# Batch 0's output projection as seven products of 256 columns per group of four feature blocks, with the orders dealt anew

## The chip, the cores and the metric

One Trainium2 chip, one core. The metric is the device time of one execution in microseconds (us): the median of 3 runs of the kernel before is 738.43 us (738.42 to 738.86).

## The reference

```python
B, H, S, Ns, D = (8, 8, 512, 32, 64)          # x: B,H,S,D   state: B,H,Ns,D
scores = scale * np.matmul(x, state.transpose(0, 1, 3, 2))
a = softmax(scores);  xread = np.matmul(a, state)
scores2 = scale * np.matmul(state, x.transpose(0, 1, 3, 2))
a2 = softmax(scores2); sread = np.matmul(a2, x)
attn_out = np.concatenate([xread, sread], axis=2)
x = attn_out.transpose(0, 2, 1, 3).reshape(B * S, H * D)    # S is 512 + 32 here
rms = np.sqrt(np.mean(x * x, axis=-1, keepdims=True) + 1e-06)
xn = x / rms * rms_g
g = xn @ w_gate                                # 512 x 1536
silu = g * (1.0 / (1.0 + np.exp(-g)))
out = (silu * (xn @ w_val) @ w_out)            # 1536 x 512
```

Tokens read from the states (cross attention), states read from the tokens, an RMS norm, and a gated feed-forward network. The three weight matrices arrive as float64; x, state and the output are float32.

## The kernel before

**Work.** A batch has 512 tokens; its 1536 hidden features are 12 feature blocks of 128, taken in six pairs `mp`. Because the tokens read from only 32 states per head, a pair's gate and value weights are first multiplied with the states (L745: "own weights", tile `v`), and the hidden layer is then a product of these with the attention weights `aT_s`. For batch 0 that is done plainly, block by block in `hidden`: two PSUM tiles `pv` for a block (L791 for block 0, in halves of 256 columns, L798 for the others, 512 columns), a silu on ScalarE into `t` (L804) and a product on VectorE into `hb` (L808). The pool of `pv` has two buffers, so a block's products need the tiles that the silu and the product of the block before have read. Batch 0's output projection is `project_as_ready`, L1005: each of the 12 blocks of `hb` times `wo`, for four rows of 128 tokens, 512 columns each, accumulated in four PSUM banks over all 12 blocks. `projected` copies these banks out on ScalarE (L1022). Batches 1 to 7 and the states use products by Strassen's scheme: seven in place of eight for the hidden layer (`hidden_seven`, L902, 256 columns each), 49 in place of 64 for the projection (`project_twice`, L1206). Their sums of weights are made at the end of batch 0's stage: `weight_sums` (L1048) and `weight_quarters` (L1160), both on VectorE; the sums of `v` (`vs`, L772 to L775) and of `aT_s` (`aT_t`, L820 to L823) are made on GpSimd.

**Weights.** The 18 pieces of 1 MB (gate, val, out for each pair in turn) are loaded by SyncE (L235), RAW_AHEAD of them ahead, and become float32 by two ScalarE passes (`lin` L268, `ex` L271, in `exponents`) and two VectorE passes (L292, L296, in `values`). The end of a piece's VectorE passes frees its buffer and issues the load of the piece RAW_AHEAD later. Gate and val of a pair go into a tile `w_m` and from there to `w_d` in DRAM, from which the later batches fetch them; the third goes to its place in `wo`.

**Order.** Every instruction's place on its engine is fixed by strings written out by hand. Each letter of such a string takes one step of a generator: in ORDER, `h`, `t`, `u` are the three parts of `hidden` for batch 0, `p` the projection, `c` its copies, `e` and `d` the two halves of the conversion, `v` the products with the states, `A` and `S` batch 1's attention, `s` the states' read of batch 0 (L629 to L699), `k` `weight_sums`, `Q` quarters, `w` batch 1's first products, `z` a matmul that only keeps TensorE awake (L1346). FIRST holds batch 1, PERIOD batches 2 to 6, LAST batch 7, STATES the states. Engines run their own queues in order and wait for one another by semaphores; `ORDER` covers about the first 124 us.

The tables `seven["c22"]`, `seven["s2"]` and `seven["k"]` are pools for the later batches' projection that are opened late, in the space that the pools of the startup (`raws`, `conv`, `x_0`) leave.

## Time and profile before

| | |
|---|---|
| median of 3 runs | 738.43 us |
| profiled execution, its own time | 738.43 us |
| span of its instructions | 736.5 us |
| granted TensorE clock | 1.000 |
| TensorE busy | 730.9 us (99%) |
| VectorE busy | 564.6 us (77%) |
| ScalarE busy | 350.2 us (48%) |
| GpSimd busy | 271.4 us (37%) |

Rows of the profile give a start and a length in us (timeline, chain of waits), or a stretch and then each engine's busy time in it with its number of instructions (windows). PE is TensorE, PEld its weight load, DVE VectorE, ACT ScalarE, POOL GpSimd, SP SyncE. A float32 matmul that the program writes once stands as two TensorE instructions in the trace: the 48 matmuls of L1005 are 96 there. A name after "<-" in brackets is what ended the idle time before the instruction.

### The profile page before, as it was taken

The numbers are of one execution on the slowest core, as the hardware profiler recorded it, in microseconds if no ns is written. First come the engines' busy times: TensorE is split into PE (matmuls) and PEld (weight loads), VectorE is DVE, ScalarE is ACT, GpSimd is POOL, SyncE is SP. The second block draws the span as 40 slices with busy tenths as digits, with TensorE's granted clock in tenths as the row PEclk, the third lists the DMA queues.
The fourth block names the chain that finished last, engine by engine and source line by source line (L and its number), as shares of the span: only waits on it lengthen the run. The fifth ranks groups of instructions, "written<-read, shape, count | busy, mean of one in ns | idle before, by whom it ended". The sixth has DMA issues, their size and how long they took to land.

```text
span 736.5 us, 14288 instructions
## 1 busy us (share of the span) xinstructions
PE 730.9 (99%) x5604; PEld 591.4 (80%) x5604; DVE 564.6 (77%) x952; ACT 350.2 (48%) x610; POOL 271.4 (37%) x362
## 2 busy tenths in 40 slices
PE   9999999999999999999999999999999999999997
PEld 7644444889978997789888987899778987899996
DVE  5885697799848994699569984899469955888852
ACT  5997923563275426553455427542655336411220
POOL 2300006521482228512753248222851277325400
PEclk9999999999999999999999999999999999999999
DMA  8989946917682297507861588229850782063411
GB/s 235 367 284 378 325 179 241 330 52 267 213 321 58 95 319 278 168 30 304 270 228 29 212 283 304 61 93 321 281 165 31 301 278 75 1 231 114 143 44 29
DMA packets 58426, 146.15 MB, mean 198 GB/s; under 512 B 10228, under 2 KB 29176, under 8 KB 51448
## 3 DMA queue, kind: packets, MB, share of 16 engines
q1 hardware_dynamic: 47312, 126.30, 48.3%
q10 hardware_dynamic: 11048, 18.95, 8.6%
q8 instruction: 44, 0.72, 0.4%
q14 instruction: 22, 0.18, 0.1%
HBM read 116.46 MB, written 28.77 MB: 197 GB/s over the span
## 4 chain that ended last, share of the span: by engine, by line
PE 98%; DMA 1%; SPq 0%; issue 0%; ACT 0%
PE f L902 40%; PE f L1206 31%; PE f L1005 6%; PE pv L798 5%; PE pv L745 4%; PE f L1068 2%; PE at L745 2%; DMA x_b<-in_x_dram 1%; PE at L450 1%; PE f L672 1%; PE at L368 1%; PE pv L791 0%; PE at L319 0%; PE at L672 0%; PE f L577 0%; PE pv L529 0%
## 5 line engine op out<-in xcount | busy, mean ns | idle before, releaser
L902 PE MATMUL f<-aT_s,v 128*128 128x256 f32 x504 | 118.8, 381 | 0.0
L902 PEld LDWEIGHTS f<-aT_s,v 128*128 128x128 f32 x504 | 94.9, 191 | 19.3 <-issue 5.3
L965 DVE TENSOR_TENSOR g<-g,f 128x512 f32<-128x512 f32 x84 | 56.1, 683 | 60.8 <-PE f L902 54.5
L1234 POOL TENSOR_TENSOR kept<-kept 128x256 f32<-128x256 f32 x28 | 24.4, 872 | 171.5 <-DVE kept L1246 112.7
L902 PE MATMUL f<-aT_t,vs 128*128 128x256 f32 x336 | 86.7, 382 | 0.0
L1206 PE MATMUL f<-w,h 128*128 128x128 f32 x588 | 75.4, 276 | 0.0
L1206 PEld LDWEIGHTS f<-w,h 128*128 128x128 f32 x588 | 70.1, 192 | 4.1 <-issue 4.1
L902 PEld LDWEIGHTS f<-aT_t,vs 128*128 128x128 f32 x336 | 62.6, 190 | 13.2 <-issue 3.1
L772 POOL TENSOR_TENSOR vs<-v 128x256 f32<-128x256 f32 x42 | 33.0, 785 | 106.7 <-ACT v L757 106.5
L1219 ACT COPY kept<-f 128x512 f32<-128x512 f32 (+1 forms) x56 | 29.3, 545 | 81.5 <-PE f L1206 58.1
L956 ACT ACTIVATE hb<-g 128x1024 f32<-128x1024 f32 x42 | 44.5, 1059 | 46.2 <-DVE g L965 46.1
L312 POOL TENSOR_TENSOR ri<-ss,mhalf 128x4 f32<-128x4 f32 (+1 forms) x9 | 9.8, 1094 | 109.8 <-ACT ss L400 104.6
L954 ACT COPY g<-f 128x512 f32<-128x512 f32 x42 | 24.6, 585 | 49.0 <-PE f L902 49.0
L757 ACT COPY v<-pv 128x512 f32<-128x512 f32 x56 | 31.0, 595 | 31.9 <-PE pv L745 31.6
L978 DVE TENSOR_TENSOR hb<-hb,f 128x512 f32<-128x512 f32 (+1 forms) x48 | 31.0, 645 | 18.1 <-PE f L902 17.8
L1005 PE MATMUL f<-wo,hb 128*128 128x512 f32 x96 | 44.1, 599 | 0.0
L902 PE MATMUL f<-aT_t,v 128*128 128x256 f32 x168 | 43.8, 383 | 0.0
L902 PE MATMUL f<-aT_s,vs 128*128 128x256 f32 x168 | 43.2, 380 | 0.0
L965 DVE TENSOR_TENSOR c<-c,f 128x512 f32<-128x512 f32 (+1 forms) x48 | 31.2, 650 | 15.1 <-PE f L902 15.0
L1206 PE MATMUL f<-wo,h 128*128 128x128 f32 x336 | 42.1, 275 | 0.0
L1206 PE MATMUL f<-wo,hb 128*128 128x128 f32 x336 | 42.1, 275 | 0.0
L1206 PEld LDWEIGHTS f<-wo,hb 128*128 128x128 f32 x336 | 39.9, 192 | 0.5
(242 smaller groups left out, 1621.3 us busy)
## 6 DMA issues: line engine op xcount, KB each, us to landing
w_m<-w_d SPq DMA_DIRECT2D x48, 1024.0 KB
w<-t_d SPq DMA_DIRECT2D x49, 576.0 KB
out_dram<-kept SPq DMA_DIRECT2D x28, 256.0 KB
raw<-in_moe_w_val_dram SPq DMA_DIRECT2D x6, 1024.0 KB
raw<-in_moe_w_out_dram SPq DMA_DIRECT2D x6, 1024.0 KB
w_d<-w_m SPq DMA_DIRECT2D x6, 1024.0 KB
x_b<-in_x_dram SPq DMA_DIRECT2D x6, 1024.0 KB
x_d<-xB ACTq DMA_DIRECT2D x6, 1024.0 KB
```

What stands on the lines that cost most here:

```text
L745: TE.matmul(out=pv[e][Ns * j:Ns * j + Ns, :], lhsT=stT_g[b][D * e:D * e + D, j, :], rhs=w[D * e:D * e + D, j].rearrange("p m k f -> p (m k ...
L757: SE.copy(v[:, e].rearrange("p m k f -> p (m k f)"), pv[e])
L772: GE.tensor_tensor(out=vs[:, 0], in0=a21, in1=a22, op=ALU.add)
L798: TE.matmul(out=to[0], lhsT=lhs(i, k), rhs=r, start=(i == 0), stop=(i == len(rhs) - 1))
L902: TE.matmul(out=ps[:, i, 0:half], lhsT=l[:, i, :], rhs=r, start=(start and i == 0 and k == 0), stop=(k == len(lhs) - 1), skip_group_check= ...
L954: SE.copy(gates(q)[1], q["x"][:, :, 0:half])
L956: SE.activation(out=hb[:, 2 * mp:2 * mp + 2, 0:n].rearrange("p m (c t) -> p m c t", c=2), in_=q["g"][:, :, :, 0:half], func=ACTF.Silu if s ...
L965: VE.tensor_tensor(out=to, in0=to, in1=q[ps][:, :, 0:half], op=ALU.add)
L978: VE.tensor_tensor(out=part, in0=part, in1=val, op=ALU.mult)
L1005: TE.matmul(out=banks[r], lhsT=hb[:, m, P * r:P * r + P], rhs=wo[:, m, :], start=(m == 0), stop=(m == NM - 1))
L1206: TE.matmul(out=to[half][:, slot, :], lhsT=lhs[:, k, :], rhs=rhs[:, k, :], start=(fresh and n in (0, 4) and k == 0), stop=(k == QM - 1), s ...
L1219: SE.copy(of_half(k, i), banks[name][i])
```

## The change

Batch 0's projection no longer runs block by block. The conversion and the hidden layer of batch 0 take the pairs in the order 0, 3, 1, 4, 2, 5 (`BLOCKS`), so that after every second pair four feature blocks are there which form a group g: blocks 2g, 2g+1 and 6+2g, 7+2g. For each of the three groups the projection is made by seven products of four matmuls each (21 products, 84 matmuls of 256 columns in place of 48 of 512); a letter of the order takes two of the four. Three of the seven go to the banks "11", "12", "21" and accumulate there over the groups. Four go one after another into one bank, "x", whose content is wanted after each of them: for group 0 ScalarE copies it out (L1075), for groups 1 and 2 VectorE adds it to what was kept (L1077). The four sums of weights of a group are made by 12 subtractions on GpSimd (L1023), one of which overwrites a quarter of `wo`; the four sums of `hb` by 12 operations on VectorE (L1033). `weight_sums` then has 9 operations in place of 12. At the end VectorE makes three sums from PSUM and GpSimd two more, and the output is stored in four pieces of 128 x 2 x 256. RAW_AHEAD is 3, `lin` has one buffer, and `en` lies in the tile "kept". ORDER, PERIOD and FIRST are dealt anew; LAST and STATES stay.

```diff
 P = 128
-RAW_AHEAD = 4
+RAW_AHEAD = 3
 W_BUFS = 3
+BLOCKS = (0, 3, 1, 4, 2, 5)
...
 ORDER = (
-    "zzzzaazaaaaggggaaazzzbzeeeaaabddaaabbeeddbbbbsssbzaaaAAAAabbdbeaaaaabAbbbAAAAAdb"
...
+    "zzzzaazaaaggggaaaaziizzbzeeeaaaddbbebbaddaabebbsssebzaaaAAAAaAAssabbdAAssdbabbaa"
...
 PERIOD = (
-    "vxahthththuhuhuthththhthhvvhaaaxxhhxxafaauuuutttuhhthhaahhuuuuttxhuhhthhauukkath"
...
+    "vahhntthhhtuuhhhnutttaahhhhaxtxvvaahhuuuaxxhuuttxthhhhthhxhaaauuuuauthfuthxxutkx"
...
 FIRST = (
-    "aaaaahtvvqqqqqqqqahathhhvtuqquxxhhtqhuhxqthutthuuhhaaahauxttqhtfuxxxhhqqhhthxuuu"
...
+    "hhaattavqvhxtaxhahhaauuuqtuqhhtqqtvhqhthhquuqquahuthtqqfuaxhhutxxqqxhthhuaahuhhu"
...
+    seven["k"] = ctx.enter_context(tc.tile_pool(name="kept", bufs=1))
+    seven["c22"] = ctx.enter_context(tc.tile_pool(name="late2", bufs=2))
+    seven["s2"] = ctx.enter_context(tc.tile_pool(name="quarters_h", bufs=2))
...
     conv = early.enter_context(tc.tile_pool(name="conv", bufs=2))
+    line = early.enter_context(tc.tile_pool(name="line", bufs=1))
...
     pieces = []
-    for mp in range(NM // 2):
+    for mp in BLOCKS:
...
         if kind == 2:
+            mp = BLOCKS[mp]
...
                     tops[k] = conv.tile([P, 8 * P], I32, name="ex")
-                    lin = conv.tile([P, 8 * P], F32, name="lin")
+                    lin = line.tile([P, 8 * P], F32, name="lin")
...
                     if k % 3 == 1:
-                        nc.sync.dma_start(out=w_d[k // 3], in_=w_sb[k // 3])
+                        nc.sync.dma_start(out=w_d[BLOCKS[k // 3]], in_=w_sb[k // 3])
...
         yield
-        en = x_0.tile([P, HT, 2, 4 * Ns], F32, name="en")
-        e = eS.rearrange("p c e j n -> p (c e j) n")
-        VE.tensor_tensor(out=en.rearrange("p c e (j n) -> p (c e j) n", n=Ns), in0=e,
-                         in1=z.unsqueeze(2).to_broadcast(e.shape), op=ALU.mult)
+        if "en" not in soft_0:
+            soft_0["en"] = seven["k"].tile([P, 2, HT, HD], F32, name="kept", tag="kept")
+        en = soft_0["en"][:, h]
+        VE.tensor_tensor(out=en.rearrange("p c (k n) -> p (c k) n", n=Ns),
+                         in0=eS.rearrange("p c e j n -> p (c e j) n"),
+                         in1=z.unsqueeze(2).to_broadcast([P, HT * 2 * 4, Ns]), op=ALU.mult)
...
             for c in range(HT):
-                TE.transpose(out=tp[:, i, c, :], in_=en[:, c, i, :], identity=ident)
+                TE.transpose(out=tp[:, i, c, :], in_=en[:, c, P * i:P * i + P], identity=ident)
...
-    def project_as_ready(banks):
-        for f in (fx, fz, fx, fy):
-            banks.append(f.tile([P, DM], F32, name="f"))
-        def part(m, r):
-            TE.matmul(out=banks[r], lhsT=hb[:, m, P * r:P * r + P], rhs=wo[:, m, :],
-                      start=(m == 0), stop=(m == NM - 1))
-        for m in range(NM - 2):
-            for r in range(4):
-                part(m, r)
-                if r % 2:
-                    yield
-        for r in range(4):
-            part(NM - 2, r)
-            part(NM - 1, r)
-            yield
+    def wo_block(g, i, j):
+        return wo[:, HM * i + 2 * g:HM * i + 2 * g + 2, HD * j:HD * j + HD]
+    def hb_block(g, i, j):
+        return hb[:, HM * j + 2 * g:HM * j + 2 * g + 2, HS * i:HS * i + HS]
+    GROUPS = HM // 2
+    group_t, group_s = {}, {}
+    def group_weights():
+        for g in range(GROUPS):
+            t = group_t[g] = seven["s2"].tile([P, 3, 2, HD], F32, name="group", tag="h2")
+            b11, b12, b21, b22 = (wo_block(g, i, j) for i in range(2) for j in range(2))
+            for to, x_, y_ in ((t[:, 0], b12, b11), (t[:, 1], b22, t[:, 0]), (b12, b22, b12),
+                               (t[:, 2], b21, t[:, 1])):
+                GE.tensor_tensor(out=to, in0=x_, in1=y_, op=ALU.subtract)
+                yield
+    def group_tokens():
+        for g in range(GROUPS):
+            u = group_s[g] = seven["s2"].tile([P, 3, 2, HS], F32, name="group", tag="h2")
+            a11, a12, a21, a22 = (hb_block(g, i, j) for i in range(2) for j in range(2))
+            for to, x_, y_, op in ((u[:, 0], a21, a22, ALU.add), (u[:, 1], u[:, 0], a11, ALU.subtract),
+                                   (a21, a11, a21, ALU.subtract), (u[:, 2], a12, u[:, 1], ALU.subtract)):
+                VE.tensor_tensor(out=to, in0=x_, in1=y_, op=op)
+                yield
+    def group_product(bank, lhs, rhs, start, stop):
+        for k in range(2):
+            for r in range(HT):
+                TE.matmul(out=bank[:, r, :], lhsT=lhs[:, k, P * r:P * r + P], rhs=rhs[:, k],
+                          start=(start and r == 0 and k == 0), stop=(stop and k == 1),
+                          skip_group_check=True)
+            yield
+    def groups_direct(banks):
+        for name, pool in (("11", fx), ("12", fz), ("21", fx)):
+            banks[name] = pool.tile([P, HT, HD], F32, name="f")
+        for g in range(GROUPS):
+            first, last = g == 0, g == GROUPS - 1
+            yield from group_product(banks["11"], hb_block(g, 0, 1), wo_block(g, 1, 0), first, last)
+            yield from group_product(banks["12"], group_s[g][:, 2], wo_block(g, 1, 1), first, last)
+            yield from group_product(banks["21"], hb_block(g, 1, 1), group_t[g][:, 2], first, last)
+    def groups_chained(banks):
+        x_ = banks["x"] = fy.tile([P, HT, HD], F32, name="f")
+        for g in range(GROUPS):
+            yield from group_product(x_, hb_block(g, 0, 0), wo_block(g, 0, 0), True, True)
+            yield from group_product(x_, group_s[g][:, 1], group_t[g][:, 1], False, True)
+            yield from group_product(x_, hb_block(g, 1, 0), wo_block(g, 0, 1), False, True)
+            yield from group_product(x_, group_s[g][:, 0], group_t[g][:, 0], False, True)
+    kept_0 = []
+    def chained_sums(banks):
+        k = seven["k"].tile([P, 2, HT, HD], F32, name="kept", tag="kept")
+        kept_0.extend([k[:, 0], k[:, 1]] + [seven["c22"].tile([P, HT, HD], F32, name="c22") for i in range(2)])
+        for g in range(GROUPS):
+            for k in kept_0:
+                if g == 0:
+                    SE.copy(k, banks["x"])
+                else:
+                    VE.tensor_tensor(out=k, in0=k, in1=banks["x"], op=ALU.add)
+                yield
     def projected(banks, store):
-        spare = seven["s"].rearrange("p (r k) f -> p r (k f)", r=3)
-        for r in range(4):
-            ot = spare[:, r] if r < 3 else two.tile([P, DM], F32, name="ot", tag="g")
-            SE.copy(ot, banks[r])
-            store(r, 0, DM, ot)
-            yield
+        k11, k12, k21, k22 = kept_0
+        VE.tensor_tensor(out=k11, in0=k11, in1=banks["11"], op=ALU.add)
+        store(0, 0, HD, k11)
+        yield
+        VE.tensor_tensor(out=k12, in0=k12, in1=banks["12"], op=ALU.add)
+        yield
+        GE.tensor_tensor(out=k12, in0=k12, in1=k21, op=ALU.subtract)
+        VE.tensor_tensor(out=k21, in0=k21, in1=banks["21"], op=ALU.add)
+        store(1, 0, HD, k21)
+        yield
+        store(1, HD, HD, k22)
+        GE.tensor_tensor(out=k12, in0=k12, in1=k22, op=ALU.add)
+        store(0, HD, HD, k12)
+        yield
...
         seven["vs"] = ctx.enter_context(tc.tile_pool(name="sums", bufs=3))
-        seven["c22"] = ctx.enter_context(tc.tile_pool(name="late2", bufs=2))
         seven["w2"] = ctx.enter_context(tc.tile_pool(name="quarters_w", bufs=3))
-        seven["s2"] = ctx.enter_context(tc.tile_pool(name="quarters_h", bufs=2))
-        seven["k"] = ctx.enter_context(tc.tile_pool(name="kept", bufs=1))
...
                 return wo[:, HM * i + k:HM * i + k + 2, HD * j:HD * j + HD]
-            for dst, a, b in ((t1[:, k:k + 2], blk(0, 1), blk(0, 0)),
-                              (t2[:, k:k + 2], blk(1, 1), t1[:, k:k + 2]),
-                              (blk(0, 1), blk(1, 1), blk(0, 1)),
-                              (t4[:, k:k + 2], blk(1, 0), t2[:, k:k + 2])):
-                VE.tensor_tensor(out=dst, in0=a, in1=b, op=ALU.subtract)
+            for dst, a, b, op in ((t2[:, k:k + 2], blk(0, 1), blk(0, 0), ALU.add),
+                                  (t1[:, k:k + 2], blk(1, 1), t2[:, k:k + 2], ALU.subtract),
+                                  (t4[:, k:k + 2], blk(1, 0), t2[:, k:k + 2], ALU.subtract)):
+                VE.tensor_tensor(out=dst, in0=a, in1=b, op=op)
...
             if b == 0:
-                rows_ = rows_.rearrange("(h p c) f -> h c p f", h=2, c=HT)
-                nc.sync.dma_start(out=rows_[r // HT, r % HT], in_=ot)
+                rows_ = rows_.rearrange("(h p c) f -> h p c f", h=2, c=HT)
+                nc.sync.dma_start(out=rows_[r], in_=ot)
...
             if m not in parts_0:
-                parts_0[m] = hidden(m, lambda e, k, m=m: v_sb[0, m // 2][0][:, e, m % 2, k, :],
+                parts_0[m] = hidden(2 * BLOCKS[m // 2] + m % 2, lambda e, k, m=m: v_sb[0, m // 2][0][:, e, m % 2, k, :],
...
-    parts_0, banks_0 = {}, []
+    parts_0, banks_0 = {}, {}
...
                "h": of_batch_0(0), "t": of_batch_0(1), "u": of_batch_0(2),
-               "p": project_as_ready(banks_0), "c": projected(banks_0, store_tokens(0)),
+               "p": groups_chained(banks_0), "r": groups_direct(banks_0), "W": group_weights(),
+               "T": group_tokens(), "x": chained_sums(banks_0), "c": projected(banks_0, store_tokens(0)),
...
         for stream in ORDER:
-            if stream in "ckw" and "s" not in seven:
+            if stream in "kw" and "s" not in seven:
...
```

Three places show what moved. The first is ScalarE's queue ahead of batch 0's first silu (L804, now L812). `xT` and `aT_s` are the tokens and the attention weights, `e` the exponentials of batch 0's states' read (L636, now L644). Before:

```order
L271 ACTIVATE ex<-lin,bounds 128x1024
L593 COPY aT_s<-at 128x2x256
L343 COPY xT<-at 128x4x128 x3
L593 COPY aT_s<-at 128x2x256
L268 ACTIVATE lin<-raw,bounds 128x1024
L757 COPY v<-f 128x512 x2
L271 ACTIVATE ex<-lin,bounds 128x1024
L804 ACT_TABLE_LOAD
L804 ACTIVATE t<-pv 128x512
```

and now:

```order
L349 COPY xT<-at 128x4x128
L644 ACTIVATE e_361,z_364<-sS,s_362 128x512
L656 COPY e_361<-at 128x512
L274 ACTIVATE lin<-raw,bounds 128x1024
L765 COPY v<-f 128x512
L277 ACTIVATE ex<-lin,bounds 128x1024
L601 COPY aT_s<-at 128x2x256
L765 COPY v<-f 128x512
L274 ACTIVATE lin<-raw,bounds 128x1024
L277 ACTIVATE ex<-lin,bounds 128x1024
L812 ACT_TABLE_LOAD
L812 ACTIVATE t<-pv 128x512
```

Ahead of the silu there now also stand the two exponentials of the states' read (one of them is the row just above the first one shown), a copy of them and one more pair of conversion passes.

The second is TensorE's queue in the middle of the stage, where a pair's products with the states (L745, now L753) are followed by hidden products (L798, now L806) and projection. Before:

```order
L745 MATMUL at<-w_m,stT_g 32x512 x8
L1005 MATMUL f<-wo,hb 128x512 x2
L798 MATMUL pv<-aT_s,v 128x512 x8
L745 MATMUL at<-w_m,stT_g 32x512 x8
L1005 MATMUL f<-wo,hb 128x512 x6
L450 MATMUL at<-aT_s,rows 64x512 x4
L450 MATMUL pv<-aT_s,rows 64x512 x4
L1005 MATMUL f<-wo,hb 128x512 x2
```

and now:

```order
L1039 MATMUL f<-wo,hb 128x256 x4
L753 MATMUL at<-w_m,stT_g 32x512 x8
L1039 MATMUL f<-wo,hb 128x256 x2
L1039 MATMUL f<-group 128x256 x4
L1039 MATMUL f<-wo,group 128x256 x4
L1039 MATMUL f<-wo,hb 128x256 x4
L1039 MATMUL f<-group,hb 128x256 x4
L806 MATMUL pv<-aT_s,v 128x512 x2
L1039 MATMUL f<-group 128x256 x4
```

The projection's products stand in lots of 2 or 4 matmuls, half a product or a whole one; those with `group` need the sums of GpSimd and VectorE, and those of bank "x" need it to have been read.

The third is VectorE's queue late in the stage, with the quarters of weights (L1160, now L1226), the products into `hb` (L808, now L816) and the large sum for batch 1's tokens (L463, now L469). Before:

```order
L1048 TENSOR_TENSOR wt<-wo,wt 128x512
L1160 TENSOR_TENSOR w_1033<-wt,w_1033 128x384 x2
L1160 TENSOR_TENSOR wt<-wt 128x3x128
L808 TENSOR_TENSOR hb<-t,pv 128x512
L1160 TENSOR_TENSOR w_1041<-wt 128x384
L1160 TENSOR_TENSOR w_1041<-wt,w_1041 128x384 x2
L808 TENSOR_TENSOR hb<-t,pv 128x512
L1160 TENSOR_TENSOR wt<-wt 128x3x128
L463 TENSOR_TENSOR aT_s<-aT_s,at 128x1024
```

and now:

```order
L1226 TENSOR_TENSOR w_1048<-wt,w_1048 128x384
L1077 TENSOR_TENSOR kept<-kept,f 128x512
L816 TENSOR_TENSOR hb<-t,pv 128x512 x2
L1033 TENSOR_TENSOR group<-hb 128x512
L1033 TENSOR_TENSOR group<-group,hb 128x512
L1033 TENSOR_TENSOR hb<-hb 128x2x256
L694 TENSOR_SCALAR sr<-at,z_751 128x64 x2
L1033 TENSOR_TENSOR group<-hb,group 128x512
L469 TENSOR_TENSOR aT_s<-aT_s,at 128x1024
L1082 TENSOR_TENSOR kept<-kept,f 128x512
L1077 TENSOR_TENSOR kept<-kept,f 128x512
```

Between the quarters and that sum there now stand the last group's four operations on `hb` and the additions from the banks.

More of the change, by code (lines that the diff above doesn't have):

```diff
@@ L26 @@
 ORDER = (
[L27 to L31 removed]
+    "zzzzaazaaaggggaaaaziizzbzeeeaaaddbbebbaddaabebbsssebzaaaAAAAaAAssabbdAAssdbabbaa"
+    "AaAsbbssvbabbebavebbvAddeAehbdhtdeeAAuAdddhAAethuvvveephtddsssWhuesehhssreddstpA"
+    "xdvveeWWWuTTrTppxTrrpvpeerrhxppddWAAAAeeddthhAeAAeddStddvvdvhhhuWWxiueppAeeAAddA"
+    "tuhheAddrtuTAeeArxTATTApApeSddSSvxrAvAAvrAppihxShAedppWtheeeuhetdxdvvvddupkkWWWk"
+    "kkkkSSShrrSSthhtAAQQQQkpQQxAWuhuTTTSSTAAwrrcppwwwwwxwQQrrSkcpSprrxcQppxwQwcQQ"
 )
 PERIOD = (
[L35 to L38 removed]
+    "vahhntthhhtuuhhhnutttaahhhhaxtxvvaahhuuuaxxhuuttxthhhhthhxhaaauuuuauthfuthxxutkx"
+    "hhtuuhkkutvxkuahhhxxtthaahhuaaathushhuuuuhtthassthhthguuuuuutuuuspphupupcpkkppck"
+    "kkklkskkgppppppkkpkffkaakaaaapppgfkpcakppppppppcckpgagkppcaakaaakskppaoaaakkkkkg"
+    "ppppppppppaaapgkkoaaoopaassssakkkkppppaapkpkosacwwxxwxxsssxflfcooxo"
 )
 FIRST = (
[L42 to L46 removed]
+    "hhaattavqvhxtaxhahhaauuuqtuqhhtqqtvhqhthhquuqquahuthtqqfuaxhhutxxqqxhthhuaahuhhu"
+    "ttthhhqhtxxuukqhkaquuGuvtxhhtaaaukxtaaaGhhtkhhxxhhhGuuuuuttutaaauhhuhuhtuhuutupp"
+    "hppppppaaaucuffupkakukkkkppcpppkkpkpppckkaakaalaakkkkkpfkpppcpassaaksaagsppcpkpk"
+    "akkkppggappppppppaoogggpsssgcppkakkpssppkooaaassppkskppakkkkoopaafpwwxxxclfwxsxx"
+    "coos"
 )
```

11 lines of the change are left out of this document (removed).

## The prediction

> **What bounds the kernel now.** I read the page's busy shares and its chain of waits first, then busy time by stage, then the chain in order of time around the projection.
>
> ```profile
> PE 730.9 (99%) x5604; PEld 591.4 (80%) x5604; DVE 564.6 (77%) x952; ACT 350.2 (48%) x610; POOL 271.4 (37%) x362
> PE 98%; DMA 1%; SPq 0%; issue 0%; ACT 0%
> 0.00:26.50 26.50, 24.81 (x201) 19.55 (x201) 15.58 (x45) 17.11 (x29) 6.93 (x27) 1.00 0.85 266
> 26.50:123.80 97.30, 97.30 (x484) 43.02 (x483) 76.44 (x119) 67.60 (x90) 13.34 (x21) 1.00 0.79 289
> 123.80:203.60 79.80, 79.80 (x670) 68.03 (x675) 65.99 (x112) 37.20 (x67) 27.95 (x37) 1.00 0.66 227
> 522.70:602.48 79.78, 79.78 (x671) 68.32 (x677) 63.73 (x106) 37.51 (x71) 35.18 (x46) 1.00 0.59 197
> 676.90:736.50 59.60, 55.72 (x421) 53.08 (x419) 32.43 (x60) 12.35 (x29) 12.68 (x13) 1.00 0.20 71
> ```
>
> TensorE sets the end: 99% of the span and 98% of the chain. The five lower rows are stages, each with its length and then the busy time of PE, PEld, DVE, ACT and POOL. From 26.5 us, where batch 0's hidden layer begins, to 123.8 us, where batch 1's begins, TensorE has no idle time at all; nor in batch 1 (the third row) or batch 6 (the fourth). So a TensorE microsecond taken out of the second row is a microsecond of the end, as long as the others bring their operands in time; and a changed order of batches 1 to 6 has nothing to win there. The second engine of the stage is VectorE, with 97.3 - 76.4 = 20.9 us of idle time. The profiled execution took 738.43 us, the median of the runs too, so the sum is made against 738.43.
>
> **TensorE's work.** The chain gives the pitch of the old product and of the new one's shape, which batches 1 to 7 use for their hidden layer:
>
> ```profile
> 33.80 5.15 PE f L1005 x12
> 131.51 15.87 PE f L902 x72
> 149.26 15.74 PE f L902 x72
> ```
>
> Each matmul of the program is two instructions here. Before: 48 matmuls, 96 x 5.15/12 = 96 x 0.429 = 41.2 us. After: 84 matmuls are 168 instructions of 256 columns, 168 x 15.74/72 = 168 x 0.2186 = 36.7 us. **-4.5 us.** Bounds: by the slower row 168 x 0.2204 = 37.0, so -4.2; the windows' third row has batch 1's 168 such instructions, in a stage without idle time, and nothing there makes them cheaper than 36.1 (0.215), so -5.1. The columns fall from 48 x 512 to 84 x 256, by an eighth, and TensorE is given no instruction of another kind, so nothing hides this term.
>
> **The start.** ScalarE's queue ahead of the first silu:
>
> ```profile
> 18.43 0.58 ACT L343 COPY xT<-at 128x512 f32<-128x512 f32 x1 [0.30 <-PE at L341]
> 22.27 1.07 ACT L343 COPY xT<-at 128x512 f32<-128x512 f32 x2 [0.57 <-PE at L341]
> 24.22 0.58 ACT L593 COPY aT_s<-at 128x512 f32<-128x512 f32 x1 [0.87 <-PE at L591]
> 29.45 0.60 ACT L804 ACTIVATE t<-pv 128x512 f32<-128x512 f32 x1 [0.17 <-PE pv L791]
> 29.94 1.25 ACT L268 ACTIVATE lin<-raw,bounds 128x1024 f32<-128x1024 int16 x1
> 31.22 1.15 ACT L271 ACTIVATE ex<-lin,bounds 128x1024 int32<-128x1024 f32 x1
> 37.31 0.72 ACT L636 ACTIVATE e<-sS,s 128x512 f32<-128x512 f32 x1
> 42.59 1.07 ACT L648 COPY e<-at 128x512 f32<-128x512 f32 x2
> 30.10 0.30 PEld L798 LDWEIGHTS pv<-aT_s,v 128*128 128x128 f32 x2 [0.23 <-ACT t L804]
> 41.72 1.04 PE L646 MATMUL at<-ident,e 128*128 128x128 f32 x8
> ```
>
> The new order puts four kinds of work of batch 0 and the conversion ahead of that silu: two exponentials (2 x 0.72), one copy of them (1.07/2 = 0.53) and one pair of conversion passes (1.25 + 1.15), 4.4 us. ScalarE's idle time there is 0.30 + 0.57 + 0.87 + 0.17 = 1.9 us. So the silu starts some 2.5 us later, and the ninth row says who waits: block 1's products need the PSUM tile that it empties. Of this, half of the eight transposes of the tenth row (0.5 us) are TensorE work done earlier. **+2.0 us.** From below 0 (the queue ahead of 17 us has room for all of it); from above 3.9 (none of the idle time takes it in). I stay at the row sum, give or take 0.9, its largest single wait.
>
> **VectorE and GpSimd.** Prices:
>
> ```profile
> L1048 DVE TENSOR_TENSOR wt<-wo x3: 681/681/683, 95.6 to 101.1; 128x512 f32<-128x512 f32 x3
> L1022 ACT COPY hs<-f x3: 585/585/587, 116.7 to 122.2; 128x512 f32<-128x512 f32 x3
> L710 POOL TENSOR_TENSOR sqT<-sqT x2: 1052/1162/1273, 636.5 to 637.8; 128x512 f32<-128x512 f32 x1, 128x256 f32<-128x256 f32 x1
> 113.47 0.55 DVE L1160 TENSOR_TENSOR wt<-wt 128x384 f32<-128x384 f32 x1
> 119.34 1.08 DVE L1160 TENSOR_TENSOR wo<-wo 128x384 f32<-128x384 f32 x1
> 115.23 0.73 POOL L820 TENSOR_TENSOR aT_t<-aT_s 128x256 f32<-128x256 f32 x1 [3.01 <-DVE aT_s L463]
> 118.96 1.04 POOL L772 TENSOR_TENSOR vs<-v 128x256 f32<-128x256 f32 x1
> 131.99 1.04 POOL L774 TENSOR_TENSOR v<-v 128x256 f32<-128x256 f32 x1
> 132.37 0.67 DVE L965 TENSOR_TENSOR g<-g,f 128x512 f32<-128x512 f32 x1
> ```
>
> VectorE gains 12 sums of `hb`, 8 additions from bank "x" and 3 from the others, and loses 3 weight sums: 20 x 0.68 = 13.6 us, into 20.9 us of idle time. ScalarE gains four copies and loses four (0.585 each): nothing. GpSimd gains 12 subtractions of 512 elements at 1.27 us, 15.2 us, where it is idle for 97.3 - 13.3 = 84 us; two more at the end. By themselves these fit. But the last six rows show the two engines hindering each other: an operation of 384 elements with both inputs in SBUF takes 0.55 us while GpSimd is idle and 1.08 beside a GpSimd addition, which itself goes from 0.73 to 1.04. With one input in PSUM (L965) VectorE keeps its 0.67 beside L774. So the 15.2 us of GpSimd work become up to 15.2 x 1.04/0.73 = 21.7 us, in which VectorE runs at 0.55/1.08 = 0.51 and loses up to 10.6 us. The stage will be 97.3 - 4.5 + 2.0 = 94.8 us. With nothing lost VectorE needs 76.4 + 13.6 = 90.0 of it, with half of that loss 95.3, with all 100.6. About half of VectorE's work in this stage has two SBUF inputs (the `or` of the conversion, the sums of weights and of `hb`), so I take the half: **+0.5 us**, with 0 below (work slips into batch 1's stage, where VectorE has 79.8 - 66.0 = 13.8 us free) and +5.8 above.
>
> The Trainium skill has a stricter rule for these pairs: SBUF — State Buffer, section "Who interferes with whom", says that a VectorE instruction with two SBUF inputs and a GpSimd instruction that reads SBUF exclude each other, and the loser is blocked for the other's whole instruction; with at most one SBUF input VectorE doesn't contend. The trace agrees on who suffers (1.08 against 0.67), not on a block by the whole 1.04 or more. By that rule alone, with each subtraction met, VectorE would lose 15.2 us, need 105.2, and the time be 738.43 - 4.5 + 2.0 + 10.4 = 746.3 (an estimate); it is the far end of the second rival below, and I give it 0.03 of that rival's chance.
>
> **The chained bank.** Each of the twelve products into "x" waits until the one before has been read. On TensorE most have other work between; the shortest cover that I find, one of the other seven products with its four matmuls, is 8 x 0.2186 = 1.75 us against a read-out of 0.59 (ScalarE) or 0.68 us (VectorE) behind what its queue holds, at worst one conversion pass:
>
> ```profile
> 93.88 1.22 DVE L296 TENSOR_TENSOR wo<-raw,ex 128x1024 int32<-128x1024 int32 x1
> ```
>
> 1.22 + 0.68 = 1.90, a shortfall of 0.15 that may come at a few places. Price 0 in the sum, since ScalarE's four reads and most of VectorE's have the queue free; from above 12 x 0.6 = 7.2, with every read-out exposed.
>
> **Loads.** With RAW_AHEAD 3 a piece is asked for when the piece three before is done. One load, alone on the queues, is issued at 73.05, and the DMA share falls back in the last window:
>
> ```profile
> 73.05 0.37 SPq L235 DMA_DIRECT2D raw<-in_moe_w_gate_dram  x1
> 73.00:74.00 1.00, 1.00 (x4) 0.52 (x3) 0.59 (x1) 0.37 (x1) 0.00 (x0) 1.00 0.04 16
> 77.00:78.00 1.00, 1.00 (x7) 0.69 (x6) 0.85 (x2) 0.98 (x3) 0.00 (x0) 1.00 0.46 176
> ```
>
> That is some 4.4 us from issue to landing. The pieces of the conversion follow each other every 4 to 6 us (18 in some 95 us), so three buffers leave two pitches, 8 us or more: 0, hidden by ScalarE's other work; at worst the tightest piece late by a microsecond or two, inside the next term's risk. One `lin` buffer keeps a pass from starting before the one that reads it is over, 0.1 us a piece, in ScalarE's 97.3 - 67.6 = 29.7 us of idle time: 0. FIRST and PERIOD: 0 by the saturated rows above; LAST and STATES are the same.
>
> **Sum:** 738.43 - 4.5 + 2.0 + 0.5 = 736.4. Own range: 738.43 - 5.1 + 1.1 + 0 = 734.4 to 738.43 - 4.2 + 2.9 + 0.9 = 738.0.
>
> **Rivals.**
>
> *No loss at the start.* ScalarE takes the earlier work into idle time, and all of TensorE's gain shows: 738.43 - 4.5 + 0.5 = 734.4, with VectorE free 733.9. For it: TensorE's 7.5 us of wake matmuls before 17 us show room in the whole stage; against it: the ninth row's wait on the silu is direct.
>
> ```profile
> 0.00:26.50 26.50, 7.52 (x20) 4.73 (x20) 1.00 0.85 266
> ```
>
> *VectorE becomes the bound (slower).* All of the 12 subtractions fall beside two-input work, at the conversion, whose weights the L745 products need, and at the sums of `hb`, which the chained products need: 738.43 - 4.5 + 2.0 + 5.8 = 741.7. It decides from the point where VectorE's need passes the 94.8 us, which the half loss already reaches; against it, VectorE's last work of the stage, the sums for batch 1's projection, can be late unpunished.
>
> *The chained bank shows (slower).* Half of the twelve read-outs exposed by 0.6 us: 738.43 - 4.5 + 2.0 + 0.5 + 3.6 = 740.0; all of them 743.6. For it: the cover of 1.75 us at two places; against it: hidden products and products with the states stand between most.
>
> *The new PERIOD makes TensorE wait.* A stage without slack on TensorE can only lose by another order; 0.35 us in each of five batches, half of a VectorE operation of 0.67, gives 736.4 + 1.75 = 738.2. For it: VectorE runs 63.7 of 79.8 us there; against it: TensorE's rows of the new order are the same work in nearly the same sequence.
>
> **How the numbers follow.** A change of 0.2% (1.48 us) is about what a measurement of this kernel can tell from none: faster is below 736.95, slower above 739.91. Forecast 0.48 (0.40 faster, 0.08 same), no loss at the start 0.12 (faster), VectorE the bound 0.18 (slower), the bank 0.11 (slower), PERIOD 0.11 (same): faster 0.52, same 0.19, slower 0.29. The time is 736.4. The range goes down to 733.6, which leaves out only the first rival with the largest TensorE gain, and up to 741.0, which takes in the bank's case and most of VectorE's, and leaves out about 0.15 above.
>
> **What would show it.** The 168 projection instructions with a pitch near 0.219 us, and batch 1's first product near 121 us, show the first term. The first silu at 31.5 to 32.3 us with block 1's products right behind it shows the second; a silu at 29.5 the first rival. TensorE idle time ended by VectorE between 30 and 125 us, with VectorE's conversion passes well over 1.22 us and its sums over 0.68 beside the new GpSimd subtractions, shows the second rival; waits of the projection's products on the copies or additions from the bank the third; idle time of TensorE repeated at the same place in each of batches 2 to 6 the last. I am wrong altogether if TensorE's stage doesn't shorten while it has no idle time, or if a conversion pass waits for its load.

## The result, and the profile after

The changed kernel takes 747.07 us (median of 5 runs, 745.34 to 748.37) against 738.44 (738.42 to 738.86): ratio 1.0112, 95% interval 1.0092 to 1.0131, 8.6 us slower. The profiled execution took 747.86 us, its span is 746.1. The page's summary and chain by engine:

```profile
PE 728.5 (98%) x5676; PEld 606.8 (81%) x5676; DVE 574.4 (77%) x972; ACT 350.6 (47%) x610; POOL 283.8 (38%) x376
PE 91%; DVE 3%; DMA 3%; ACT 1%; SPq 0%; issue 0%; POOL 0%; DVEq 0%; ACTq 0%
```

TensorE's busy time fell only from 730.9 to 728.5 us, and other engines have come into the chain. The view of what TensorE waited for (total us, times, longest) has the place, of the changed kernel:

```profile
PE f L1039 <- DVE hb L816: 9.2, 1, 9.2
PE f L325 <- POOL ri L318: 1.1, 1, 1.1
PE at L753 <- DVE w_m L302: 0.9, 1, 0.9
PE f L910 <- ACT c L960: 0.3, 1, 0.3
```

One wait of 9.2 us is more than the whole loss. Its timeline on VectorE and then on TensorE (start, length; in brackets the idle time before and who ended it):

```profile
95.52 1.23 DVE L302 TENSOR_TENSOR wo<-raw,ex 128x1024 int32<-128x1024 int32 x1
96.66 0.68 DVE L816 TENSOR_TENSOR hb<-t,pv 128x512 f32<-128x512 f32 x1
108.62 1.46 DVE L1114 TENSOR_TENSOR wt<-wo 128x512 f32<-128x512 f32 x1 [11.28 <-PE pv L806]
110.11 1.29 DVE L1114 TENSOR_TENSOR wt<-wo,wt 128x512 f32<-128x512 f32 x2
...
118.51 1.28 DVE L816 TENSOR_TENSOR hb<-t,pv 128x512 f32<-128x512 f32 x2
```

```profile
106.53 1.88 PE L806 MATMUL pv<-aT_s,v 128*128 128x512 f32 x4
...
119.24 3.78 PE L1039 MATMUL f<-wo,hb 128*128 128x256 f32 x8 [9.22 <-DVE hb L816]
122.82 2.70 PE L1039 MATMUL f<-group 128*128 128x256 f32 x8
125.45 1.09 PE L753 MATMUL pv<-w_m,stT_g 64*32 64x512 f32 x16
```

VectorE, which the prediction feared to be overfull, does nothing for 11.28 us: its first weight sum (L1114) waits for the last hidden product, whose result it does not read. Then it does ten us of sums, and behind them stand the last two products into `hb` (L816), for which TensorE waits. The first lots of products after the wait take 3.78 and 2.70 us in place of the 1.89 that eight such instructions take elsewhere in this stage. The windows (stretch, its length, busy time of five engines, granted clock, DMA) show the clock:

```profile
112.00:114.00 2.00, 0.00 (x0) 0.00 (x0) 1.97 (x5) 0.00 (x0) 0.00 (x0) 1.00 0.01 4
116.00:118.00 2.00, 0.00 (x0) 0.00 (x0) 1.97 (x5) 0.00 (x0) 0.00 (x0) 0.50 0.66 267
122.00:124.00 2.00, 2.00 (x6) 1.64 (x5) 2.00 (x5) 0.00 (x0) 0.00 (x0) 0.50 0.55 189
126.00:128.00 2.00, 2.00 (x35) 0.83 (x20) 2.00 (x4) 1.32 (x3) 1.56 (x3) 1.00 0.68 167
```

It goes to 0.50 some 4 us into the wait and comes back some 5 us after work returns: (3.78 - 1.89) + (2.70 - 1.89) = 2.7 us more. Batch 1's first product starts at 134.45 us against 123.8 before, 10.65 us later. The sum of what the rows give for these 10.65 us: -4.5 (projection) + 2.8 - 0.5 (start; the silu at 32.24 against 29.45, less work drawn forward) + 0.9 (`w_m`) + 9.2 + 2.7 = +10.6. Batches 2 to 6 then take 1.4 us less (the later orders, below). That leaves 9.3 us, against 9.6 between the spans of the two traces (746.1 and 736.5).

Why does a weight sum wait for a hidden product? Where the pools lie gives a reason (bytes in a partition, from the built programs):

```
before   raws 145664-178536 (4 buffers)   v_0 178560-186752
         late: wt 145664-164096, hs 164096-170240, aT_t 170240-173312
changed  raws 166144-190792 (3 buffers)   v_0 190816-199008
         late: wt 166144-184576, hs 184576-190720, aT_t 190720-193792
```

The pool `late` is opened when the startup's pools close and takes their space. With four raw buffers it lay inside them; VectorE itself had read them last. With three it reaches 2976 bytes (193792 - 190816) into `v_0`, the products of batch 0 with the states. Only `aT_t` lies there, but `wt`, the first tile taken from the pool, now waits for the readers of `v_0` too: the hidden products of batch 0, to the last.

### The profile page after: what moved, and what is told of

The parts are those of the page before. It is cut to its first block, busy times and chain, and to the rows that moved or that the text cites. A ratio compares the mean times of both kernels' runs of the same rounds, so it can differ in the third digit from the quotient of the medians.

```text
span 746.1 us, 14468 instructions
## 1 busy us (share of the span) xinstructions
PE 728.5 (98%) x5676; PEld 606.8 (81%) x5676; DVE 574.4 (77%) x972; ACT 350.6 (47%) x610; POOL 283.8 (38%) x376
## 4 chain that ended last, share of the span: by engine, by line
PE 91%; DVE 3%; DMA 3%; ACT 1%; SPq 0%; issue 0%; POOL 0%; DVEq 0%; ACTq 0%
PE f L910 39%; PE f L1272 31%; PE f L1039 5%; PE pv L806 4%; PE pv L753 4%; PE f L1134 2%; PE at L753 2%; DMA raw<-in_moe_w_val_dram 1%; DMA x_b<-in_x_dram 1%; PE at L456 1%; PE at L374 1%; PE f L680 1%; DVE wt L1114 1%; DMA out_dram<-c 1%; DVE w_m L302 1%
## 5 line engine op out<-in xcount | busy, mean ns | idle before, releaser
L910 PE MATMUL f<-aT_s,v 128*128 128x256 f32 x504 | 120.1, 382 | 0.0
L910 PEld LDWEIGHTS f<-aT_s,v 128*128 128x128 f32 x504 | 94.6, 190 | 23.0 <-DVE c L973 5.9
L1300 POOL TENSOR_TENSOR kept<-kept 128x256 f32<-128x256 f32 x28 | 21.2, 756 | 210.7 <-DVE kept L1312 147.1
L910 PE MATMUL f<-aT_t,vs 128*128 128x256 f32 x336 | 86.6, 381 | 0.0
L910 PEld LDWEIGHTS f<-aT_t,vs 128*128 128x128 f32 x336 | 63.1, 190 | 10.9 <-issue 1.0
L780 POOL TENSOR_TENSOR vs<-v 128x256 f32<-128x256 f32 x42 | 31.3, 746 | 88.5 <-ACT v L765 88.3
L765 ACT COPY v<-pv 128x512 f32<-128x512 f32 x56 | 31.1, 594 | 39.9 <-PE pv L753 39.6
L910 PE MATMUL f<-aT_s,vs 128*128 128x256 f32 x168 | 43.3, 380 | 0.3 <-ACT c L960 0.3
L910 PE MATMUL f<-aT_t,v 128*128 128x256 f32 x168 | 43.2, 380 | 0.0
L806 PE MATMUL pv<-aT_s,v 128*128 128x512 f32 x88 | 40.3, 597 | 0.0
L1272 PEld LDWEIGHTS f<-wo,h 128*128 128x128 f32 x336 | 39.8, 192 | 0.0
L986 DVE TENSOR_TENSOR hb<-hb,c 128x512 f32<-128x512 f32 (+1 forms) x48 | 32.9, 685 | 5.7 <-ACT hb L964 4.9
```

Source lines behind the costliest of these rows:

```text
L765: SE.copy(v[:, e].rearrange("p m k f -> p (m k f)"), pv[e])
L780: GE.tensor_tensor(out=vs[:, 0], in0=a21, in1=a22, op=ALU.add)
L806: TE.matmul(out=to[0], lhsT=lhs(i, k), rhs=r, start=(i == 0), stop=(i == len(rhs) - 1))
L910: TE.matmul(out=ps[:, i, 0:half], lhsT=l[:, i, :], rhs=r, start=(start and i == 0 and k == 0), stop=(k == len(lhs) - 1), skip_group_check= ...
L986: VE.tensor_tensor(out=part, in0=part, in1=val, op=ALU.mult)
L1272: TE.matmul(out=to[half][:, slot, :], lhsT=lhs[:, k, :], rhs=rhs[:, k, :], start=(fresh and n in (0, 4) and k == 0), stop=(k == QM - 1), s ...
```

## The experiments

**The pool alone.** `aT_t` moves into a pool of its own; every address stays.

```diff
         seven["late"] = ctx.enter_context(tc.tile_pool(name="late", bufs=1))
+        seven["turned"] = ctx.enter_context(tc.tile_pool(name="turned", bufs=1))
...
-        tt = aT_t[b] = seven["late"].tile([P, 3, HS], F32, name="aT_t")
+        tt = aT_t[b] = seven["turned"].tile([P, 3, HS], F32, name="aT_t")
```

> The changed kernel with one edit: aT_t lies in a pool of its own, opened between the pool of wt and hs and that of v, so that all addresses stay. Theory (space): VectorE's first weight sum waits 11.3 us, to 108.5 us, because the pool that holds wt is 27.6 KB a partition and reaches past the three raw buffers (24.6 KB) into the buffers of v of batch 0, which the last hidden product reads; the pool of wt and hs alone is 24.6 KB and ends where the raw buffers end. Then that wait, TensorE's 9.2 us behind it and the 2.8 us of products at a lower clock after it go: 747.1 - 9.2 - 2.8 = 735.1, 734 to 737. Rival (VectorE is the bound through its added work and GpSimd): the wait only moves, the time stays above 742.

Measured: 735.94 us (10 runs, 734.51 to 739.54) against 738.96; ratio 0.9963, interval 0.9951 to 0.9975. In its timeline the sum follows the conversion at once, and TensorE's waits of 9.2 and 0.9 us are gone:

```profile
95.83 0.68 DVE L816 TENSOR_TENSOR hb<-t,pv 128x512 f32<-128x512 f32 x1
96.42 1.45 DVE L1115 TENSOR_TENSOR wt<-wo 128x512 f32<-128x512 f32 x1
97.91 2.24 DVE L1115 TENSOR_TENSOR wt<-wo,wt 128x512 f32<-128x512 f32 x2
```

```profile
29.61:121.60 91.99, 91.99 (x557) 56.35 (x550) 82.25 (x118) 63.98 (x84) 28.95 (x31) 1.00 0.79 282
```

TensorE is busy for all 91.99 us from the first hidden product to batch 1, which starts at 121.60. The theory of space holds, and the rival that VectorE sets the time falls: the same sums and the same additions are done here.

**The sums later, pools as they are.** In ORDER the letters `k` (weight sums) and the first `Q` (quarters) move behind the last products into `hb` and the last group's operations (here and below, only the part of the string that changes):

```diff
-upkkWWWkkkkkSSShrrSSthhtAAQQQQkpQQxAWuhuTTTSSTAAwrrcpp
+upWWWSSShrrSSthhtAApxAWuhuTTTSSTAAkkkkkkkQQQQkQQwrrcpp
```

> The changed kernel with another edit: its pools as they are, but in ORDER the weight sums (k) and the first quarters (Q) stand behind the last products into hb and the last group's operations on hb. Theory (space): the wait for the last hidden product costs nothing there, since VectorE has nothing else to do before it; some 735 to 738, the later figure if the sums then delay the additions from the banks. Rival (VectorE is the bound): as before, above 742.

Measured: 747.03 us, ratio 1.0121 (1.0105 to 1.0136): missed. The wait for space no longer stops TensorE, but VectorE's gap stays empty and the 12 us of sums now stand ahead of the reading of bank "x", on which the chained products wait (the view of TensorE's waits, then VectorE's timeline with its gap and one of the sums):

```profile
PE f L1039 <- DVE kept L1077: 9.5, 1, 9.5
```

```profile
96.98 0.17 DVE L673 RECIPROCAL z<-z 128x2 f32<-128x2 f32 x1
105.52 0.69 DVE L1077 TENSOR_TENSOR kept<-kept,f 128x512 f32<-128x512 f32 x1 [8.37 <-PE f L1039]
118.52 1.20 DVE L1114 TENSOR_TENSOR wt<-wo 128x512 f32<-128x512 f32 x1
```

By its time this edit does not part the theories, since the rival had over 742. Its trace shows where the time goes: to sums that no longer stand in VectorE's gap. They are slower there, too. The third row, a weight sum, takes 1.20 us, where this kind of sum takes 0.68 to 0.69 in the changed kernel while GpSimd is idle; here GpSimd is busy for 4.92 of the 5 us from 115 on. So the two engines' hindering, the ground of the prediction's second rival, is part of this run's cost.

**The sums dealt between the read-outs,** the other repair by order alone:

```diff
-upkkWWWkkkkkSSShrrSSthhtAAQQQQkpQQxAWuhuTTTSSTAAwrrcppwwwwwxwQQrrSkcpSprrxcQppxwQwcQQ
+upWWWSSShrrSSthhtAApxAWuhuTTTSSTAAwrrcppwwwwwxkkkkwrrSckkkpSprrxckkQppxQQQQQQQQwQwcQQ
```

> The changed kernel, its pools as they are, with the weight sums (k) dealt between the last additions from the banks, each behind one that TensorE waits for, and the quarters (Q) behind them, up to batch 1's first products. Space and place together: no wait for the last hidden product and no read-out of bank x behind the sums, so batch 1 begins near 122 us; but VectorE's 12 us of sums, which fitted into its 11 us gap before, then stand ahead of batch 1's own operations, and TensorE waits there instead, some 5 to 8 us: 740 to 745. If another order alone were enough: 735 to 737. If the sums' place were of no account (rival: VectorE's total sets the time): 747.

Measured: 747.4 us, ratio 1.0115 (1.0098 to 1.0132): the figure of the rival, not the 740 to 745 of the forecast. TensorE's waits are in the forecast places, 8.2 us together, and two falls of the clock (0.72 and 0.51 in 5 us windows) add what the forecast lacked (the view of waits, then a row of TensorE's timeline behind the shorter wait):

```profile
PE f L910 <- DVE g L973: 5.6, 1, 5.6
PE f L1039 <- DVE c L1077: 2.6, 1, 2.6
124.01 3.44 PE L1039 MATMUL f<-group 128*128 128x256 f32 x8 [2.58 <-DVE c L1077]
```

Batch 1's first product starts at 127.25, not near 122. That VectorE's total sets the time does not follow from the rival's figure: with the own pool VectorE has the same work, and the time is 735.94. So in neither of two places did the sums fit once VectorE's gap was lost.

**The clock.** First try: 20 matmuls that nothing reads, ahead of the waiting product, into a tile of the pool of `pv`.

```diff
-AAwrrcpp
+AAwZZZZZZZZZZZZZZZZZZZZrrcpp
```

> The changed kernel with 20 matmuls of 256 columns that nothing reads, on TensorE ahead of the product that waits 9.2 us for hb (20 x 0.437 = 8.7 us). Theory (the clock): the wait stays, but the granted clock stays at 1.00 after it and the 2.8 us of slower products go: 747.1 - 2.8 = 744.3, and the runs agree more closely. Rival (the products after the wait are slow because their operands are late): 747 as it is, or a little more.

Measured: 754.74 us, ratio 1.0221 (1.0208 to 1.0234). This says nothing on the clock: the tile that the pool gave was the one that the late product into `hb` reads, so the matmuls waited with the rest and came on top.

```profile
PE pv L1421 <- DVE hb L817: 9.2, 1, 9.2
```

Second try, without a new tile:

```diff
         rp = along_rows(ri, NC)
+        if b == 1:
+            for again in range(20):
+                for c in range(NC):
+                    TE.transpose(out=rp[:, P * c:P * c + P], in_=ri[:, c:c + 1].to_broadcast([P, P]), identity=ident)
```

> The changed kernel with the rows of batch 1's norm (L325) written 20 more times by TensorE into the tile that they stand in, 80 small products of 0.11 us, 8.7 us, which wait for nothing. They lie in TensorE's 9.2 us of waiting for hb. Theory (the clock falls after some us without work on TensorE): the wait stays and the clock stays at 1.00, so the 2.8 us of slower products go, 747.1 - 2.8 = 744.3. Rival (the products after the wait are slow for another reason): 747.

Measured: 746.86 us (746.04 to 749.5), ratio 1.0118 (1.0102 to 1.0134), against 744.3 by the theory and 747 by the rival. In place, the theory holds: with 8.9 us of small products in the gap the clock stays at 1.00 and the products after it take 1.99 us in place of 3.78.

```profile
110.24 8.90 PE L415 MATMUL at<-ident,ri 128*128 128x128 f32 x80
119.62 1.99 PE L1043 MATMUL f<-wo,hb 128*128 128x256 f32 x8 [0.48 <-DVE hb L820]
121.67 1.99 PE L1043 MATMUL f<-group 128*128 128x256 f32 x8
```

Batch 1's first product starts 1.9 us earlier (132.59). But the time is the same within the spread: 1.1 us came back in two waits at batch 1's first products (1.4 us together, 0.3 before), and in the profiled execution, the slowest of the five, the clock was at 0.78 and 0.88 in the 5 us windows from 25 and 30 us, where TensorE waits at the start. So the 2.7 us are shown where they arise; that the end would be earlier by as much without them is not shown.

**The later orders alone.** The kernel before with the changed kernel's FIRST and PERIOD:

> The kernel before with the changed kernel's FIRST and PERIOD alone. The traces have 79.5 us from one batch to the next in batches 2 to 6 of the changed kernel against 79.8: theory, the new PERIOD gains 5 x 0.28 = 1.4 us, 737.0. Rival (the recorded prediction: no idle time there, nothing to gain): 738.4; its own rival (new waits): over 738.4.

Measured: 737.36 us, ratio 0.9978 (0.997 to 0.9987): about 1.6 us faster. The prediction had 0. The chains (start, us, what, instructions) of the kernel before, then of the changed kernel, show the same place of one batch and the next, and the small product of the norm in between:

```profile
204.88 10.55 PE f L902 x48
284.67 10.55 PE f L902 x48
355.47 0.24 PE at L395 x2
```

```profile
297.28 8.71 PE f L910 x40
366.08 0.13 PE at L401 x2
376.79 8.71 PE f L910 x40
```

A batch takes 79.51 in place of 79.79 us, 5 x 0.28 = 1.4. TensorE was busy in both. 0.11 of the 0.28 is this one product, which takes less in its new place. Another 0.16 lies in the 168 instructions of the hidden layer (L902, now L910): the chains of one batch have 36.90 us for them in the kernel before and 36.74 in the changed one. In the trace of the run itself the five batches save less, 1.0 us; the rest lies ahead of them, 0.5 of it already at batch 1's first product (123.30 against 123.80).

**The first stage without the later orders.** The own pool, with FIRST and PERIOD of the kernel before:

> The changed kernel with aT_t in its own pool (735.9 by the run above) and with FIRST and PERIOD of the kernel before: the first stage's change alone, without the wait for space. If the gains add, 735.9 + 1.6 (what the new FIRST and PERIOD gave in the kernel before) = 737.5, that is 1.4 below before: -4.5 of TensorE's work and +2 to +3 of the start. Rival (the two belong together, since ORDER leaves another state at its end): 736 or less, or over 739.

Measured: 745.61 us, ratio 1.0099 (1.0084 to 1.0113), where 737.5 was expected if the gains add. They do not: on VectorE the turned tokens of the next batch (xB) come behind the quarters, and ScalarE's queue stands at the transfer that sends them off, with the copy that TensorE waits for behind it:

```profile
PE f L910 <- ACT c L960: 6.7, 1, 6.7
```

**Three raw buffers** in the kernel before, with `aT_t` in its own pool:

```diff
-RAW_AHEAD = 4
+RAW_AHEAD = 3
```

> The kernel before with RAW_AHEAD 3 and aT_t in its own pool (else the weight sums would wait there too). The recorded prediction has 0 for three buffers: 738.4 to 739.5. Rival (a load takes up to 9.2 us from issue to landing beside others, as the changed kernel's trace shows for one piece, and two pitches do not cover it): TensorE waits at the products of own weights, 740 or more.

Measured: 745.46 us, ratio 1.0086 (1.0071 to 1.0101): the rival. One piece, issued at 52.50 us, takes 9.79 us; ScalarE and then TensorE wait, and the clock falls (timelines of the two, and the window).

```profile
62.31 1.25 ACT L268 ACTIVATE lin<-raw,bounds 128x1024 f32<-128x1024 int16 x1 [3.81 <-DMA raw<-in_moe_w_val_dram]
```

```profile
66.14 1.96 PE L745 MATMUL at<-w_m,stT_g 64*32 64x512 f32 x16 [3.58 <-DVE w_m L296]
```

```profile
60.00:70.00 10.00, 6.42 (x25) 1.95 (x25) 3.21 (x5) 4.22 (x6) 0.00 (x0) 0.74 0.87 308
```

A second wait, of 1.3 us, stands in the view of TensorE's waits. So in the old order the fourth buffer is worth 6.6 us; the new ORDER, with its own pool, runs on three without that wait.

**The start.** Three tries to take back the 2.3 us, all with the own pool. First the states' read of batch 0, a pair of conversion passes and a piece's second half moved behind the first silu:

> The changed kernel with aT_t in its own pool and, in ORDER, the states' read of batch 0 (its maxima, exponentials and the copies after them) and one pair of conversion passes behind the first silu again, the conversion of the second piece behind batch 0's first norm. Theory (the start costs what ScalarE's and VectorE's queues got ahead of the first silu): the silu comes some 2.3 us earlier, 735.9 - 2.3 = 733.6. Rival (conversion and loads that come later make TensorE wait in their turn): 735.5 or more.

Measured: 751.83 us, ratio 1.0173 (1.0153 to 1.0192). The late conversion made the first products of own weights wait 2.1 us for `w_m` and block 1 wait 4.0 us for `hb`, and the clock fell to 0.64 from 30 to 35 us and to 0.55 from 40 to 45. Mended:

> As the start restored before (aT_t in its own pool; the states' read of batch 0, one pair of conversion passes and the conversion of the second piece later), with three mendings: the first products of own weights behind the first rows of the norm, the product into hb ahead of the conversion that waits for the late pair, the states' read spread out. Theory (the start's 2.3 us come from what stands ahead of the first silu): 735.9 - 2.3 = 733.6. Rival (conversion that is later makes TensorE wait, as in the run before): 738 or more.

Measured: 750.89 us, ratio 1.0166 (1.015 to 1.0181). TensorE waits 4.5 us for `w_m` and 2.8 us for the silus, and the clock is at 0.50 from 55 to 60 us. And the states' read alone:

> The changed kernel with aT_t in its own pool and only the states' read of batch 0 (maxima, exponentials, copies, products) moved behind the first silu; the conversion stays. Theory: of the 2.3 us the part of the exponentials, the copy and the maxima goes, 1.0 to 2.0: 734 to 735. Rival: the read, being later, makes TensorE or VectorE wait elsewhere, 736 or more.

Measured: 749.17 us, ratio 1.0141 (1.0128 to 1.0155): missed as well. Here the start does what was expected (ScalarE's timeline, then TensorE's waits): the silu comes at 30.67 us against 32.50 with the own pool alone, the product behind it at 31.32 against 33.17. But between 45 and 60 us TensorE waits three times (the first, third and fourth row of the second view). For the 3.1 us, `w_m`, the load comes late: ScalarE idles 3.91 us for it. The other two, 2.3 and 1.7 us, are for a copy (L765) that stands behind the exponentials that left the start, and for a copy (L656) that left it itself. The granted clock is 0.50 from 55 to 60 us.

```profile
30.67 0.60 ACT L812 ACTIVATE t<-pv 128x512 f32<-128x512 f32 x1
```

```profile
PE at L753 <- DVE w_m L302: 3.3, 2, 3.1
PE pv L806 <- ACT t L812: 3.0, 4, 1.7
PE at L654 <- ACT v L765: 2.3, 1, 2.3
PE at L654 <- ACT e L656: 1.7, 1, 1.7
```

In these three orders the start's 2.3 us came back as waits further on. None of the three kept a gain; that another order could was not settled.

**Awake at the start.** The own pool, with two matmuls that nothing reads (`zz`) ahead of the rows of batch 0's norm:

> The changed kernel with aT_t in its own pool and two matmuls that nothing reads (0.86 us) on TensorE ahead of the rows of batch 0's norm, where it waits 1.1 us for GpSimd. Theory (the runs of the kernel with its own pool spread from 734.5 to 739.5 because the clock falls for some us after the start in some executions): the spread shrinks to under 2 us and the median comes to 735.3 or less. Rival: the spread has another source, or two matmuls are too few: 735.9 with the same spread.

Measured: 735.72 us (5 runs, 735.26 to 736.49), ratio 0.9962 (0.995 to 0.9975). The spread is 1.2 us in place of 5.0, but from half as many runs, and the 5.0 rest on one run of 739.54, without which it is 2.1; the median did not come to 735.3. So the theory is not shown. What speaks for it: in the traces of two other runs, the repeated rows and the sums dealt between, the clock was at 0.50 for 3.4 us from 27.8 and 28.8 us on, within or just behind the same wait of 1.1 us, at which the changed kernel's trace shows no fall. This and the own pool are the fastest versions, and beat both kernels.

## Why the prediction was wrong, step by step

**TensorE's work: right.** In the changed kernel's chain 36 of the projection's instructions follow each other in 8.10 us and 8 in 1.73, 0.225 and 0.216 each (0.219 was taken), and with the own pool batch 1 starts at 121.60 us; "near 121" was forecast, 123.8 it was.

**The start: right in size, half right in cause.** The silu came at 32.24 us, 2.8 late less 0.5 of work drawn forward, for +2.0. ScalarE was ready at 32.0, but TensorE, too, came only then, held by VectorE's queue through the first rows (1.1 us behind `ri`): both queues had been filled.

**VectorE and GpSimd: +0.5 was 0, and the chief rival was wrong.** With the own pool VectorE is busy 82.25 of 91.99 us, and 74.84 of the next 79.4 (65.99 of 79.8 before), and TensorE does not wait in the stage. Idle time of VectorE took the sums in. The price of the two engines' meeting was real, though: the first weight sum takes 1.45 us beside this row, of the kernel with the own pool:

```profile
96.05 1.27 POOL L1023 TENSOR_TENSOR group<-wo,group 128x512 f32<-128x512 f32 x1 [3.16 <-DVE wo L302]
```

GpSimd ends at 97.32, 0.90 after VectorE began at 96.42, and VectorE ends 0.55 after that. At half speed it would have had only some 0.2 left (an estimate: 0.68 - 0.90 x 0.51); alone it takes 0.68. This one meeting comes closer to the stricter rule that the prediction weighed (the Trainium skill, SBUF — State Buffer, "Who interferes with whom": the loser is blocked for the whole instruction) than to half speed. Here it cost the end nothing; where the sums stood elsewhere, it lengthened them (the sums later, above).

**The chained bank: 0 was right** in the changed order; the sums placed ahead of its reading show what it costs otherwise, 9.5 us.

**Loads: 0 was wrong.** It was 0.9 us in the changed kernel, 0 with the own pool in its profiled execution, and 6.6 us (745.46 - 738.82) in the old order. The 4.4 us were measured on a load that ran alone; among others a load took 9.24 us here, and 9.79 with three buffers in the old order.

**FIRST and PERIOD: 0 was wrong by 1.6 us to the good** (1.0 to 2.2 by the interval). That TensorE is busy all the time says nothing on how long the same instructions take in another sequence.

**The step that failed** is the sentence that puts VectorE's 13.6 us "into 20.9 us of idle time", where "by themselves these fit": it took for granted that the weight sums may begin when their operands are there, as in the kernel before. The amount was right, as the own pool shows; but in the changed kernel 11.28 us of that idle time stood where no sum could start. Of RAW_AHEAD 3 the prediction priced the loads, not the space: the smaller buffers no longer cover the pool that is laid over them, and the sums wait for the last hidden product. The wait itself cost 9.2 us and the fall of the clock 2.7. The terms that it had give 736.4; the kernel with that one wait removed takes 735.9. That these lie so close is in part luck. By its trace that kernel reaches batch 1 2.2 us earlier than the kernel before, of which the prediction had 2.0 (with 0.5 of loss that did not come, and 0.3 less at the start than came), and takes 1.4 less after it, which the prediction did not have; and the median of its runs lies 1.2 above the run that was traced.

## What to carry to other kernels

When a buffer count or a pool's place changes, look at what lies where and at who reads that space last: a tile can wait for work that has nothing to do with its operands, and with queues in a fixed order all that stands behind it waits too. Idle time of an engine is only room for new work if that work may start there; when the gap was lost, neither of two other places for the sums was free. A stall of TensorE can cost its clock as well, here 2.7 us on top of 9.2; waits of 2.6 us (the sums dealt between) and 3.6 us (three raw buffers) were followed by a fall too.

## What the runs showed of the hardware

The granted clock was still 1.00 in the window from 2 to 4 us into the wait and 0.50 from 6 us on; after work began at 119.24 us it was 0.50 up to 124, 0.78 in the next microsecond and 1.00 from 125. Small products that only rewrite a tile kept it at 1.00.

In windows of 0.2 us over the traces above, every stretch at half clock behind a wait lasts 3.4, 6.8 or 10.2 us: 3.4 with the repeated rows, 6.8 with three raw buffers, 10.2 in the changed kernel (from 114.2 to 124.4 us), with the sums later and with the states' read later. These are one, two and three times 3.41. So how long the products are slow does not follow from the length of the wait alone: behind 9.2 us of waiting the clock came back 5.2 us after work began, behind the 2.6 us of the sums dealt between 3.8 us after it (fall at 124.4, return at 127.8).

The Trainium skill (TensorE: Matmul & The Clock Gate, "What's actually happening") gives a window of about 3.4 us for the fall and for the return. The length of these stretches agrees. That a fall takes a whole window without work is not borne out: it came within or just behind waits of 1.1 and 2.6 us (the repeated rows, the sums dealt between).
